# Six weight loads held back in the list that orders a kernel, with new ranks for loads, conversion and masks

## The chip, the cores and the metric

The kernel runs on one core of one Trainium2 chip. The metric is the device time of one execution in microseconds (us). Lines of the kernel (L320) are counted in each kernel's own text, so the same line has a slightly other number in each.

## The reference

```python
# q, k, v: (batch 8, heads 8, seq 576, head_dim 64); tau = 0.02
scores = scale * np.matmul(q, k.transpose(0, 1, 3, 2))
thresh = np.max(scores, axis=-1, keepdims=True) - tau
scores = np.where(scores >= thresh, scores, -1e9)
scores = scores - np.max(scores, axis=-1, keepdims=True)
attn = np.exp(scores); attn = attn / (np.sum(attn, axis=-1, keepdims=True) + 1e-09)
attn_out = np.matmul(attn, v)
# x = attn_out as (8*576, 512); w_in (512, 2048), w_out (2048, 512), given in double precision
h = x @ w_in
out = (h * (1.0 / (1.0 + np.exp(-1.702 * h)))) @ w_out
```

So there are 32 pairs of heads, four to a batch, and 9 blocks of 512 tokens of feed-forward. The first block needs pairs 0 to 3 and the weights. The weights come as 64-bit numbers, and the kernel takes them apart into 32-bit ones on the chip: 32 pieces of 128 x 512, each with two loads of 512 KB, four VectorE operations and one on ScalarE. Pieces 0 to 15 are of w_in, 16 to 31 of w_out.

## The kernel before

The kernel doesn't emit its instructions in the order of the text. It makes a list of tasks with an engine, an assumed cost, a rank, what they come after, and which buffers they take and give. A small loop then plays the list in an assumed time. Whenever an engine is free, it takes the ready task of lowest rank whose buffers are free, and only then is the task's function called, which emits its instructions:

```python
def task(engine, cost, rank, f, *a, after=(), take=(), give=(), lag=0.06):
    ...
    tasks.append((engine, cost, rank, f, a, [x for x in after if x is not None], take, give, lag))
    return len(tasks) - 1
...
            for rank, i in sorted(queue):                 # in run_in_order()
                take = tasks[i][6]
                if all(free[pool] >= take.count(pool) for pool in set(take)):
                    break
            ...
            heapq.heappush(events, (now + tasks[i][1], 0, i))
            tasks[i][3](*tasks[i][4])                      # emits the instructions
```

What comes out is the order of the instructions on each engine. The waits on the chip are put in afterwards, from which instruction writes and reads which buffer.

A piece is converted in one of six places: four quarters of w_out that are not filled yet, and two separate buffers.

```python
def stage(i):                       # STAGES = 4
    if i < n_in:
        return i % (STAGES + 2) if i % (STAGES + 2) < STAGES else None
    ...
for i in range(len(pieces)):
    rank = 3.61 + 0.42 * i / n_in if i < n_in else 4.11 + 0.57 * (i / n_in - 1)
    x = stage(i)
    place = ("w64",) if x is None else (f"stage{x}",)
    a = task("POOL", 2.4, rank, load_w, i, take=place, lag=5.0)
    e = task("DVE", 0.43, rank, cv_ex, i, after=[a])
    m = task("ACT", 0.79, rank, cv_power, i, after=[e])
    a = task("DVE", 1.14, rank, cv_frac, i, after=[e])
    ...
    ready_w.append(task("DVE", 0.7, rank - 1.01, cv_end, i, after=[a, m] + over, give=place))
```

For each pair n, q and k are loaded by SyncE, transposed on VectorE (`prep`), multiplied into scores on TensorE, copied out by ScalarE, and their maxima are taken on VectorE. For the first eight pairs the threshold then goes through DRAM to reach all partitions: `row_out` writes 4.5 KB, `row_in` reads it back spread out to 576 KB and twice 144 KB, and VectorE subtracts it. Masks and exponentials follow on ScalarE.

```python
lq = task("SP", 2.0, r - 2.0, load_qk, n, 0, q0, take=own(n, "raw0"), lag=2.0)
...
pk = task("DVE", 0.77, r, prep, n, 1, after=[lk], take=own(n, "qkT1"), give=own(n, "raw1"))
...
a = task("SP", 0.35, r, row_out, n, after=[a], lag=2.3)
m = task("SP", 1.5, r, row_in, n, after=[a], take=own(n, "mb") + ("mbt",), give=("row",), lag=4.0)
```

Of the kernel before, what the change touches and what calls it, by code (L numbers as in the profile page):

```python
# [30 lines left out]
def kernel(  # L31
# [33 lines left out]
    NKT = 4  # L65
# [18 lines left out]
    psA = ctx.enter_context(tc.tile_pool(name="psA", bufs=3, space=bass.MemoryType.PSUM))  # L84
# [6 lines left out]
    kd = const.tile([P, P], FP32, name="kd")  # L91
    v_t = [const.tile([P, 2, D], FP32, name=f"v_t{i}") for i in range(2)]
# [13 lines left out]

    tasks = []
    limits = {"psA": 3, "psM": 2, "s_m": 8, "s_t": 2, "io": 2, "xT": 3, "mb": 1,
              "raw0": 1, "raw1": 1, "qkT0": 1, "qkT1": 1, "v_m": 2, "w64": 2, "mbt": 1, "row": 1, "kd": 1}
    for x in ("raw0", "raw1", "qkT0", "qkT1", "mb"):  # L110
        limits[x + "_apart"] = 1
    limits["s_m_apart"] = NKT
# [6 lines left out]
        "exps": 0.63,  # L119
        "load_qk": -0.91,  # L120
        "prep": -1.45,
        "load_v": 0.65,
        "over_groups": -1.04,
        "sub": -0.29,
    }
# [2 lines left out]
    def task(engine, cost, rank, f, *a, after=(), take=(), give=(), lag=0.06):  # L128
        if 0 <= rank < LAST:
            rank += (EARLY if a[0] < 2 * NPAIR else LATER).get(f.__name__, 0.0)  # L130
        tasks.append((engine, cost, rank, f, a, [x for x in after if x is not None],
                      take, give, lag))
        return len(tasks) - 1
# [67 lines left out]
    def own(n, *pools):  # L201
        return tuple(x + "_apart" for x in pools) if n in APART else pools
# [33 lines left out]
    n_in = len(pieces)  # L236
# [7 lines left out]
    def stage(i):  # L244

        if i < n_in:
            return i % (STAGES + 2) if i % (STAGES + 2) < STAGES else None
        i -= n_in
        return STAGES - 1 if i % 3 == 0 and i < NFC - PER_STAGE else None
# [281 lines left out]
    def cuts(b):  # L531

        return sorted({0, SH, S} | {x for x in range(-b * S % BLK, S, BLK)})
# [89 lines left out]
    BY_DMA = 8  # L623
    LEAD = 6

    ready_w = []
    for i in range(len(pieces)):
        rank = 3.61 + 0.42 * i / n_in if i < n_in else 4.11 + 0.57 * (i / n_in - 1)
        if not wide:
            ready_w.append(task("POOL", 1.2, rank, load_w, i, lag=2.5))  # L630
            continue
        x = stage(i)
        place = ("w64",) if x is None else (f"stage{x}",)
        a = task("POOL", 2.4, rank, load_w, i, take=place, lag=5.0)
        e = task("DVE", 0.43, rank, cv_ex, i, after=[a])
        m = task("ACT", 0.79, rank, cv_power, i, after=[e])
        a = task("DVE", 1.14, rank, cv_frac, i, after=[e])

        over = [ready_w[y] for y in range(i) if i >= n_in and stage(y) == (i - n_in) // PER_STAGE]
        ready_w.append(task("DVE", 0.7, rank - 1.01, cv_end, i, after=[a, m] + over, give=place))  # L640

    warm = task("ACT", 1.5, -2.0, first_act)
    tau_done = task("DVE", 1.0, -2.0, tau_terms, after=[warm])
# [41 lines left out]
    for n in range(NP):  # L685
        gate = per_pair * (n - LEAD)
        after = ffn[gate : gate + 1] if gate >= 0 else []
        r = float(n)

        slow = 1.2 if n < NPAIR else 1.0  # L690
        q0, q1 = (nc.sync, nc.scalar) if n == 0 else (nc.sync, nc.sync)
        lq = task("SP", 2.0, r - 2.0, load_qk, n, 0, q0, take=own(n, "raw0"), lag=2.0)
        lk = task("SP", 2.0 if n else 0.1, r - 2.0, load_qk, n, 1, q1, take=own(n, "raw1"), lag=2.0)
        lv = task("SP", 2.1, r - 1.2, load_v, n, take=("v_m",), lag=2.0)
        pq = task("DVE", 0.77, r, prep, n, 0, after=[lq], take=own(n, "qkT0"), give=own(n, "raw0"))
        pk = task("DVE", 0.77, r, prep, n, 1, after=[lk], take=own(n, "qkT1"), give=own(n, "raw1"))
        pd = task("ACT", 0.5, r, prep_kd, n, after=[pk], take=("kd",))
        mx = []
        for t in range(NKT + 1):
            tail = t == NKT  # L700
            copies = []
            for c in range(1 if tail else 2):

                a = task(
                    "PE", (0.97 if tail else 0.53) * slow, r, scores, n, t, c,
                    after=[pq, pk] + ([pd] if tail else []) + after,
                    take=("psA", "s_t") if tail else ("psA",) + (own(n, "s_m") if c == 0 else ()),
                    give=own(n, "qkT0", "qkT1") + ("kd",) if tail else (),
                )
                after = [a]  # L710
                copies.append(task("ACT", 0.65, r, keep, n, t, c, after=[a], give=("psA",)))
            mx.append(task("DVE", 0.76 if tail else 1.37, r, in_groups, n, t, ALU.max, after=copies))
        a = task("DVE", 0.78, r, over_tiles, n, ALU.max, after=mx)
        a = task("DVE", 0.78, r, over_groups, n, ALU.max, after=[a])
        if n < BY_DMA:
            a = task("DVE", 0.5, r, lower_rows, n, after=[a, tau_done], take=("row",))
            a = task("SP", 0.35, r, row_out, n, after=[a], lag=2.3)
            m = task(
                "SP", 1.5, r, row_in, n, after=[a], take=own(n, "mb") + ("mbt",), give=("row",),
                lag=4.0,  # L720
            )
        else:
            a = task("DVE", 0.7, r, lower, n, after=[a, tau_done])
            m = task("DVE", 1.38, r, spread_max, n, after=[a], take=own(n, "mb"))
        ws, subs = [], [m]
        for t in range(NKT + 1):
            tail = t == NKT
            a = task(
                "DVE", (0.76 if n < BY_DMA else 1.5) if tail else 1.36, r, sub, n, t, after=subs[-1:],
                give=own(n, "mb") + (("mbt",) if n < BY_DMA else ()) if tail else (),  # L730
            )
            subs.append(a)
            a = task("ACT", 0.68 if tail else 1.16, r, mask, n, t, after=[a])
            ws.append(task("ACT", 0.87 if tail else 1.34, r, exps, n, t, after=[a]))
        back = own(n, "s_m") * NKT + ("s_t",)
        every = range(NKT + 1)
        if n < NPAIR:

            pv = den = None
            for t in every:  # L740
                first = t == 0
                den = task(
                    "PE", 1.1 * slow, r, sums_by_pe, n, [t], True, after=[ws[t], den],
                    take=("psM", "psM") if first else (),
                )
                pv = task(
                    "PE", 1.1 * slow, r, values, n, [t], after=[ws[t], den, pv, lv],
                    take=("psA",) if first else (), give=(back[t],) if t < NKT else ("s_t", "v_m"),
                )
            a = task("DVE", 1.22, r, one_row, n, after=[den], give=("psM", "psM"))  # L750
        else:
            pv = task("PE", 4.85, r, values, n, every, after=ws + [lv], take=("psA",), give=("v_m",))
        if NPAIR <= n < BY_PE:
            a = task("PE", 5.2, r, sums_by_pe, n, every, False, after=ws + [pv], take=("psA",), give=back)
            a = task("DVE", 1.22, r, one_row, n, after=[a], give=("psA",))
        elif n >= BY_PE:
            su = [
                task("DVE", 0.76 if t == NKT else 1.37, r, in_groups, n, t, ALU.add, after=[ws[t]])
                for t in range(NKT + 1)
            ]  # L760
            a = task("DVE", 0.78, r, over_tiles, n, ALU.add, after=su + [pv], give=back)
            a = task("DVE", 0.78, r, over_groups, n, ALU.add, after=[a])
            a = task("DVE", 0.7, r, one_group, n, after=[a])
        a = task("DVE", 1.07, r, spread_sums, n, after=[a])
        b, hp = divmod(n, NPAIR)
        new = {(b * S + x) // BLK for x in cuts(b)[:-1]} if hp == 0 else set()
        if b:
            new -= {(b * S - 1) // BLK}
        placed[n] = task(
            "DVE", 1.1, r, place_x, n, after=[a, pv], take=("xT",) * len(new), give=("psA",)  # L770
        )
        while hp == NPAIR - 1 and (next_blk + 1) * BLK <= (b + 1) * S:
            feed_forward(next_blk)
            next_blk += 1
# [31 lines left out]
```

## Time and profile before

| | before |
|---|---|
| time | 1435.12 us, median of 3 (1434.89 to 1436.98) |
| span of the profiled run | 1431.2 us |
| TensorE busy, idle | 1380.6, 50.6 us |
| of the idle time, in the first 126 us | 41.2 us |
| first feed-forward matmul; pair 3 placed | 117.8; 118.8 us |
| longest wait of VectorE in the front | 11.7 us, for q of pair 1 |

From 240 us to the end TensorE is idle for only 3.9 us. The time is therefore decided in the front, before the first block of feed-forward runs without gaps, and at one later wait for w_out. The lines themselves are in the prediction.

### The profile page before, as it was taken

To read this page: it belongs to the slowest core of one execution; us is meant where nothing else is said; L and a number is where in the kernel's file an instruction comes from. 1 tells how busy PE (TensorE), PEld (TensorE's weight loads), DVE (VectorE), ACT (ScalarE), POOL (GpSimd) and SP (SyncE) were. 2 spreads that over 40 slices of the span, in tenths; PEclk is the share of its full clock that TensorE was granted. 3 is DMA by queue.
4 is the path that set the end of the run, shared out by engine and by line. 5 is a ranking of instruction groups with operands and counts; after the bars stand their busy time and mean duration, and the time that the engine had idled before them with its cause. 6 is when DMAs were issued, how large, how long until landed. Compare 5 with 4: busy or idle time off the path is not lost.

```text
span 1431.2 us, 13710 instructions
## 1 busy us (share of the span) xinstructions
PE 1380.6 (96%) x4936; PEld 650.2 (45%) x4936; DVE 970.2 (68%) x1629; ACT 658.9 (46%) x886; POOL 35.8 (3%) x78
## 2 busy tenths in 40 slices
PE   3779989999999999999999999999999999999998
PEld 2344434444444444444444444444444444444443
DVE  3999999888778888888887887788778710100200
ACT  3786655555455555555555554455445500100100
POOL 2012220000000000000000000000000000000000
PEclk8999999999999999999999999999999999999999
DMA  9468673211111111111111111111110000000000
GB/s 246 99 191 259 204 254 94 67 33 25 33 40 33 26 25 40 33 33 25 33 40 33 25 31 34 40 25 25 33 40 8 1 8 22 0 7 22 0 7 22
DMA packets 205707, 79.31 MB, mean 55 GB/s; under 512 B 192840, under 2 KB 192840, under 8 KB 205640
## 3 DMA queue, kind: packets, MB, share of 16 engines
q1 hardware_dynamic: 196072, 44.60, 14.4%
q0 software_dynamic: 7200, 33.55, 6.6%
q8 instruction: 39, 0.64, 0.2%
q10 hardware_dynamic: 2368, 0.30, 0.1%
q14 instruction: 28, 0.23, 0.1%
HBM read 68.93 MB, written 9.47 MB: 55 GB/s over the span
## 4 chain that ended last, share of the span: by engine, by line
PE 88%; DVE 6%; SPq 2%; DMA 2%; ACT 1%; issue 1%; DVEq 0%; ACTq 0%
PE ops L574 34%; PE hps L555 34%; PE pv L476 9%; PE ps L344 9%; PE ps L337 2%; SPq L214 2%; DVE s_m L447 1%; DVE part L377 1%; DMA mb<-row 1%; ACT gT L462 1%; ACT gT L458 1%; DMA row<-flat 0%; PE den L476 0%; DVE w_in L309 0%; DVE gT L447 0%
## 5 line engine op out<-in xcount | busy, mean ns | idle before, releaser
L574 PE MATMUL ops<-w_out,gT 128*128 128x512 f32 x1152 | 507.8, 596 | 5.0 <-DVE w_out L309 5.0
L555 PE MATMUL hps<-xT,w_in 128*128 128x512 f32 x1152 | 506.4, 595 | 0.3 <-DVE gT L566 0.3
L377 DVE TRANSPOSE_TENSOR_REDUCE part<-s_m 128x36 f32<-128x1152 f32 x228 | 303.5, 1358 | 101.8 <-ACT s_m L363 96.8
L574 PEld LDWEIGHTS ops<-w_out,gT 128*128 128x128 f32 x1152 | 216.2, 190 | 273.8 <-issue 263.5
L555 PEld LDWEIGHTS hps<-xT,w_in 128*128 128x128 f32 x1152 | 216.3, 190 | 267.9 <-issue 256.4
L566 DVE SCALAR_TENSOR_TENSOR gT<-th,hps 128x512 f32<-128x512 f32 x144 | 97.5, 677 | 234.8 <-ACT th L563 234.2
L363 ACT COPY s_m<-ps 128x576 f32<-128x576 f32 x240 | 138.8, 650 | 155.4 <-PE ps L344 153.9
L563 ACT ACTIVATE th<-hps 128x512 f32<-128x512 f32 x144 | 85.2, 592 | 217.4 <-PE hps L555 191.6
L458 ACT ACTIVATE s_m<-s_m 128x1152 f32<-128x1152 f32 x120 | 137.6, 1153 | 62.5 <-DVE s_m L447 62.1
L462 ACT ACTIVATE s_m<-s_m,shift,scl 128x1152 f32<-128x1152 f32 x120 | 160.5, 1343 | 2.4
L447 DVE TENSOR_TENSOR s_m<-s_m,mb 128x1152 f32<-128x1152 f32 x120 | 156.2, 1351 | 5.0 <-DMA mb<-row 4.3
L344 PE MATMUL ps<-qkT 64*128 64x288 f32 x960 | 144.6, 432 | 12.7 <-DVE qkT L320 12.2
L581 ACT ACTIVATE osb<-ops 128x512 f32<-128x512 f32 x36 | 21.4, 594 | 233.5 <-PE ops L574 233.3
L344 PEld LDWEIGHTS ps<-qkT 64*128 64x128 f32 x960 | 83.9, 189 | 91.4 <-issue 52.5
L476 PE MATMUL pv<-s_m,v_m 128*64 128x288 f32 x960 | 124.9, 413 | 0.0
L476 PEld LDWEIGHTS pv<-s_m,v_m 128*64 128x64 f32 x960 | 67.2, 138 | 64.0 <-issue 12.6
L377 DVE TRANSPOSE_TENSOR_REDUCE part_t<-s_t 128x18 f32<-128x576 f32 x59 | 44.2, 749 | 0.7 <-ACT s_t L363 0.2
L543 DVE TENSOR_TENSOR xT<-pv,rc 128x288 f32<-128x288 f32 (+8 forms) x96 | 28.3, 350 | 17.0 <-PE pv L476 15.7
L337 PE MATMUL ps<-qkT,kd 128*128 128x288 f32 x120 | 36.8, 429 | 0.3 <-ACT s_m L363 0.3
L476 PE MATMUL pv<-s_t,v_t 128*64 128x288 f32 x256 | 36.5, 406 | 0.0
L452 DVE TENSOR_TENSOR s_t<-s_t,mb 64x576 f32<-64x576 f32 x48 | 36.0, 749 | 0.3
L325 ACT COPY kd<-qkT 64x64 f32<-64x64 f32 x60 | 14.5, 241 | 45.6 <-DVE qkT L320 45.2
(81 smaller groups left out, 621.4 us busy)
## 6 DMA issues: line engine op xcount, KB each, us to landing
out_dram<-osb SPq DMA_DIRECT2D x36, 256.0 KB, 2.0
q_raw<-in_q_dram SPq DMA_DIRECT2D x120, 72.0 KB, 2.2
k_raw<-in_k_dram SPq DMA_DIRECT2D x116, 72.0 KB, 2.3
v_m<-in_v_dram SPq DMA_DIRECT2D x64, 128.0 KB, 2.4
w_out<-in_moe_w_in_dram POOLq DMA_DIRECT2D x12, 512.0 KB, 9.1
w<-in_moe_w_out_dram POOLq DMA_DIRECT2D x12, 512.0 KB, 4.8
w_out<-in_moe_w_in_dram POOLq DMA_DIRECT2D x12, 511.6 KB, 10.0
w64s<-in_moe_w_out_dram POOLq DMA_DIRECT2D x12, 511.6 KB, 5.8
```

Source lines behind the costliest of these rows:

```text
L337: nc.tensor.matmul(ps[:, i, 0:SH], lhsT=kd, rhs=qT[:, ts(i, SH)], start=True, stop=True,)
L344: nc.tensor.matmul(ps[:, h, 0:SH], lhsT=kT[ts(h, D), ts(t, P)], rhs=qT[ts(h, D), ts(c, SH)], start=True, stop=True,)
L363: nc.scalar.copy(out=o, in_=pss.pop((n, t, c))[:, :, 0:SH])
L377: nc.vector.tensor_reduce(out=o, in_=i, axis=AXL.X, op=op, apply_transpose=True)
L447: nc.vector.tensor_tensor(out=s, in0=s, in1=mb, op=ALU.subtract)
L458: nc.scalar.activation(out=s, in_=s, func=AF.Prelu, alpha=STEEP)
L462: nc.scalar.activation(out=s, in_=s, func=AF.Exp, scale=scl, bias=shift)
L476: nc.tensor.matmul(o[c][ts(h, D), 0:SH], lhsT=lhsT, rhs=rhs, start=(t == 0), stop=(t == NKT),)
L555: nc.tensor.matmul(hidden[j], lhsT=w_in[:, c, ts(j, P)], rhs=xTs[blk][:, c, :], start=(c == 0), stop=(c == NDC - 1),)
L563: nc.scalar.activation(out=ths[j], in_=hidden[j], func=AF.Tanh, scale=GELU_SCALE / 2)
L566: nc.vector.scalar_tensor_tensor(out=gT[j], in0=ths.pop(j), scalar=1.0, in1=hidden.pop(j), op0=ALU.add, op1=ALU.mult)
L574: nc.tensor.matmul(acc[i], lhsT=gT[j][:, ts(i, P)], rhs=w_out[:, j, :], start=(j == 0), stop=(j == NFC - 1),)
```

## The change

Its intent: six weight loads are held back until k of the third and fourth pair (pairs 2 and 3) is transposed, and loads and conversion get other ranks. The mask moves behind the exponentials, and the list learns of three buffers that it did not count.

```diff
-              ... "kd": 1}
+              ... "kd": 1, "rc": 1, "v_t0": 1, "v_t1": 1}
...
-        "load_v": 0.65,
+        "load_v": 1.46,
+        "mask": 1.27,
...
-        rank = 3.61 + 0.42 * i / n_in if i < n_in else 4.11 + 0.57 * (i / n_in - 1)
+        rank = 3.41 + 0.67 * i / n_in if i < n_in else 4.4 + 0.36 * (i / n_in - 1)
...
         a = task("POOL", 2.4, rank, load_w, i, take=place, lag=5.0)
+        w_loads.append(a)
...
-        ready_w.append(task("DVE", 0.7, rank - 1.01, cv_end, i, ...))
+        ready_w.append(task("DVE", 0.7, rank - 2.28, cv_end, i, ...))
...
         pk = task("DVE", 0.77, r, prep, n, 1, after=[lk], ...)
+        if n in (2, 3):
+
+            for a in w_loads[3 * (n - 2) : 3 * (n - 1)]:
+                tasks[a][5].append(pk)
...    (take and give of "rc" and of the tail of v, cut)
```

More of the change, by code (lines that the diff above doesn't have):

```diff
@@ L108 @@
     limits = {"psA": 3, "psM": 2, "s_m": 8, "s_t": 2, "io": 2, "xT": 3, "mb": 1,
-              "raw0": 1, "raw1": 1, "qkT0": 1, "qkT1": 1, "v_m": 2, "w64": 2, "mbt": 1, "row": 1, "kd": 1}
+              "raw0": 1, "raw1": 1, "qkT0": 1, "qkT1": 1, "v_m": 2, "w64": 2, "mbt": 1, "row": 1, "kd": 1, "rc": 1, "v_t0": 1, "v_t1": 1}
     for x in ("raw0", "raw1", "qkT0", "qkT1", "mb"):
@@ L624 @@
     LEAD = 6
-    ready_w = []
+    ready_w, w_loads = [], []
     for i in range(len(pieces)):
-        rank = 3.61 + 0.42 * i / n_in if i < n_in else 4.11 + 0.57 * (i / n_in - 1)
+        rank = 3.41 + 0.67 * i / n_in if i < n_in else 4.4 + 0.36 * (i / n_in - 1)
         if not wide:
@@ L639 @@
         over = [ready_w[y] for y in range(i) if i >= n_in and stage(y) == (i - n_in) // PER_STAGE]
-        ready_w.append(task("DVE", 0.7, rank - 1.01, cv_end, i, after=[a, m] + over, give=place))
+        ready_w.append(task("DVE", 0.7, rank - 2.28, cv_end, i, after=[a, m] + over, give=place))
     warm = task("ACT", 1.5, -2.0, first_act)
@@ L693 @@
         lk = task("SP", 2.0 if n else 0.1, r - 2.0, load_qk, n, 1, q1, take=own(n, "raw1"), lag=2.0)
-        lv = task("SP", 2.1, r - 1.2, load_v, n, take=("v_m",), lag=2.0)
+        v_tail = f"v_t{n % 2}"
+        lv = task("SP", 2.1, r - 1.2, load_v, n, take=("v_m", v_tail), lag=2.0)
         pq = task("DVE", 0.77, r, prep, n, 0, after=[lq], take=own(n, "qkT0"), give=own(n, "raw0"))
         pk = task("DVE", 0.77, r, prep, n, 1, after=[lk], take=own(n, "qkT1"), give=own(n, "raw1"))
+        if n in (2, 3):
+            for a in w_loads[3 * (n - 2) : 3 * (n - 1)]:
+                tasks[a][5].append(pk)
         pd = task("ACT", 0.5, r, prep_kd, n, after=[pk], take=("kd",))
@@ L747 @@
                     "PE", 1.1 * slow, r, values, n, [t], after=[ws[t], den, pv, lv],
-                    take=("psA",) if first else (), give=(back[t],) if t < NKT else ("s_t", "v_m"),
+                    take=("psA",) if first else (), give=(back[t],) if t < NKT else ("s_t", "v_m", v_tail),
                 )
@@ L751 @@
         else:
-            pv = task("PE", 4.85, r, values, n, every, after=ws + [lv], take=("psA",), give=("v_m",))
+            pv = task("PE", 4.85, r, values, n, every, after=ws + [lv], take=("psA",), give=("v_m", v_tail))
         if NPAIR <= n < BY_PE:
@@ L763 @@
             a = task("DVE", 0.7, r, one_group, n, after=[a])
-        a = task("DVE", 1.07, r, spread_sums, n, after=[a])
+        a = task("DVE", 1.07, r, spread_sums, n, after=[a], take=("rc",))
         b, hp = divmod(n, NPAIR)
@@ L769 @@
         placed[n] = task(
-            "DVE", 1.1, r, place_x, n, after=[a, pv], take=("xT",) * len(new), give=("psA",)
+            "DVE", 1.1, r, place_x, n, after=[a, pv], take=("xT",) * len(new), give=("psA", "rc")
         )
```

## The prediction

> **What bounds the kernel now.** I read the page's engine totals and its 40 slices first. One slice is 1431.2 / 40 = 35.8 us.
>
> ```profile
> PE 1380.6 (96%) x4936; PEld 650.2 (45%) x4936; DVE 970.2 (68%) x1629; ACT 658.9 (46%) x886; POOL 35.8 (3%) x78
> ...
> PE   3779989999999999999999999999999999999998
> ...
> DVE  3999999888778888888887887788778710100200
> ```
>
> TensorE is idle for 1431.2 - 1380.6 = 50.6 us in all, and the digits put nearly all of it into the first four slices. Nothing that is done about weights, loads or ranks can shorten the saturated part; it can only shorten the front. So I took the windows of the front (columns: window, its length, then busy us of PE, PEld, DVE, ACT, POOL, then the granted clock, DMA share, GB/s).
>
> ```profile
> 0.00:18.00 18.00, 7.52 (x34) 5.29 (x35) 3.87 (x10) 6.56 (x12) 8.23 (x26) 1.00 0.96 288
> 18.00:36.00 18.00, 6.86 (x36) 4.70 (x35) 8.80 (x17) 6.15 (x13) 0.00 (x0) 0.72 0.85 201
> 36.00:54.00 18.00, 10.69 (x66) 5.76 (x67) 15.46 (x23) 15.28 (x22) 0.00 (x0) 0.91 0.50 109
> 54.00:72.00 18.00, 15.61 (x118) 8.26 (x116) 17.79 (x26) 12.82 (x13) 1.04 (x2) 1.00 0.37 89
> 72.00:90.00 18.00, 12.00 (x82) 6.95 (x80) 16.94 (x29) 14.25 (x23) 1.09 (x3) 0.95 0.68 193
> 90.00:108.00 18.00, 16.62 (x116) 8.37 (x114) 17.37 (x37) 14.62 (x17) 2.12 (x4) 0.86 0.55 183
> 108.00:126.00 18.00, 15.54 (x96) 8.42 (x94) 16.93 (x35) 14.16 (x22) 6.48 (x13) 1.00 0.66 224
> ```
>
> PE is busy for 84.8 of these 126 us, so 41.2 of the 50.6 idle us lie here. There are two regimes. From 36 to 126 us VectorE is the bound: 84.5 of 90 us busy, while it does the maxima and the subtraction for pairs 0 to 3 and the first weight conversions. From 0 to 36 us VectorE itself is starved: 12.7 of 36 us busy, 23.3 us idle, and the DMA engines are at 96% and 85%. The feed-forward matmuls, which then keep TensorE full to the end, need xT of pair 3; VectorE places it at 118.8 us. Time lost by VectorE before 36 us is therefore lost by the whole kernel. The waits of VectorE up to 37 us say for what:
>
> ```profile
> DVE gT L320 <- DMA gT<-in_q_dram: 11.7, 1, 11.7
> DVE neg L607 <- DMA tau_b<-in_tau_dram: 6.0, 1, 6.0
> DVE part L377 <- ACT s_m L363: 2.8, 1, 2.8
> DVE qkT L320 <- DMA q_raw<-in_q_dram: 2.2, 1, 2.2
> DVE gT L320 <- DMA gT<-in_k_dram: 0.3, 1, 0.3
> ```
>
> The big one, 11.7 us, is pair 1's q (pairs 1 and 3 live in the gT space). The chain and the DMA queues in 9 to 27 us show why it is late: SyncE's issue of pair 1's q, normally about 0.5 us for each of four transfers, takes 15.5 us, because the DMA engines are full of weights (queue, packets, MB, share of the 16 engines).
>
> ```profile
> 7.38 7.92 SPq L214
> ...
> 15.34 6.25 SPq L214
> ...
> q0 software_dynamic: 1121, 5.25, 74.3%
> q1 hardware_dynamic: 4662, 0.72, 23.7%
> ```
>
> And these weights are not needed then. Six pieces (two 512 KB transfers each) are fetched by 26 us, one is touched by an 0.39 us operation at 10.35 us, and the rest wait for VectorE: the next weight load waits 56.5 us for a free place, and the first conversion is finished at about 70 us.
>
> ```profile
> 70.96 0.53 POOL L272 DMA_DIRECT2D w_out<-in_moe_w_in_dram  x1 [56.50 <-DVE w_out L283]
> ```
>
> **What the Trainium skill says.** "DMA: Bandwidth & Descriptors", section "Issuing engines are not separate DMA queues": transfers started from SyncE, ScalarE and GpSimd run on the same 16 engines and interleave. The trace agrees: GpSimd's queue took 74.3% of the engines' time, SyncE's 23.7%, and it was SyncE's issue that stretched. The same page, "Queues, rings and completion order", says that an engine takes turns between its queues packet by packet; large weight packets against 128-byte pieces of q and k would then give the weights most of the time, as seen. "TensorE: Matmul & The Clock Gate", Part 1, says that the clock is released after some 3.4 us of sustained work and falls back when idle. The trace agrees: the 32 score matmuls of pair 0 took 7.04 us (220 ns each) and those of pair 1, after an 11.1 us gap, 6.00 us (188 ns), while 12 later ones took 1.73 us (144 ns).
>
> **The change, part by part.**
>
> 1. The hold. The six loads go behind the transpose of k of pair 2 (three) and of pair 3 (three). No instruction is added; bytes and conversions stay. First, pair 0: q and k needed 24.2% + 23.4% of the first 9 us of all engines = 4.3 us of DMA time, and weights took another 40.5%. Without them the pair should land before VectorE's last tau operation ends (6.8 us), so its transposes start at about 6.9 instead of 8.99: 2.1 us. Its scores and copies then take as long as now (from the end of k's transpose at 10.4 to the last copy's end at 19.6: 9.2, less one 0.74 us conversion on ScalarE that no longer lies among them): from 8.3 to about 16.8. Second, pair 1: SyncE reaches its q at 6.6 us as now, issues q and k in 2.06 us each (as for pair 2 now: 26.95 and 29.11) and they land 2.4 us later, at about 13. So its transposes fit into the holes between pair 0's maxima and its scores follow pair 0's on a warm TensorE. Third, VectorE: last maximum 0.73 us, then the reduction to the threshold row, 2.4 us now (32.79 to 34.99) and say 2.9 with waits, then pair 2's transposes 1.4 us: it reaches pair 1's maxima at about 16.8 + 0.7 + 2.9 + 1.4 = 21.9 instead of 36.33. **That is 14.4 us.**
>
> 2. A further 2.06 us idle before the first subtraction now (43.51, waiting for the threshold row from DRAM, 5.5 us of DMA) can go, since VectorE will have pair 1's whole chain to do. But the first three weight loads start at about 22 us and run against just that row: at 147.45, with busy engines, the row took 6.3 us instead of 3.8. I count +1 us of the 2.
>
> 3. Are the weights late now? Pieces 0 to 2 are issued at about 22 us and 3 to 5 at about 30; the landing is 3.6 to 13 us in this trace, so all six are there by about 42. The first conversion moves from 68.5 to about 53. They still wait for VectorE: cost 0.
>
> 4. The new ranks. Finishing a conversion earlier frees its place and so starts the next load earlier; the ranks of w_out, the later v, and the masks behind the exponentials on ScalarE shift order only. They bear on one visible wait:
>
> ```profile
> PE ops L574 <- DVE w_out L309: 5.0, 1, 5.0
> ```
>
> At 208.4 us TensorE outruns the last w_out conversions, whose loads (203.7 to 214.7) wait for conversion places. Earlier finishes argue for less of it; the later rank of w_out (4.4 and on, before 4.11 and on) argues for more. I count +2 us of the 5, and my uncertainty here is 5 us either way.
>
> 5. The extra limits on rc and on the tail of v name buffers that have 1 and 2 copies anyway; they should order nothing differently: 0.
>
> Sum: 14.4 + 1 + 0 + 2 = about 17 us, 1435.1 - 17 = 1418.
>
> **The rivals.** (a) The gain is eaten on the way: the front stays bound by VectorE, but weight loads now start 20 us later and the feed-forward waits for w_in. In favour: 16 pieces, 16.8 MB, before the last first-layer weights; at the 190 to 220 GB/s of the windows that is some 80 us, so from 22 us on they would be all there only at about 102, near the new start of feed-forward (118 - 15). Against: even now only six places are held before 70 us and feed-forward begins with 9 of 16 pieces finished, so the early fetch bought nothing. If true, half the gain: 1427. (b) The conversions come at worse moments after the new ranks: the 5.0 us wait grows to 10 and TensorE gets other holes between 120 and 240 us, where VectorE is still 95% busy. Then 1424 to 1430. (c) The order gets much better than I can see: VectorE's remaining 5.5 us of idle time from 36 to 126 us and the whole 5.0 us stall go too: 1435 - 16.5 - 5 - 4 = 1409. (d) The hold has no effect because pair 1's q was limited by SyncE's own issue of small packets. Against: pair 2's q took 2.06 us when weights had landed. I give it very little; then 1435.
>
> **Range and chances.** The front's 14 us rests on durations in the trace, the rest is order. I take 1418, with 1409 (rival c) to 1428 (rivals a and b). Over 2% faster needs 1406.4, that is 28.7 us, out of 41.2 + 5.6 us of idle TensorE in the first 240 us; VectorE has some 97 us of work to do before feed-forward and cannot begin before 6 us, so feed-forward can hardly begin before 103 instead of 118 unless work is also moved behind it. So 5%. Slower by 2% needs the order to break badly: 1%.
>
> **What would show it.** Right: the 11.7 us wait for pair 1's q is under 1 us; pair 0's first transpose starts at about 7 us and pair 1's maxima at about 22; VectorE is busy for over 22 us in the first 36; feed-forward's first matmul comes at about 102 to 105 us, and TensorE is full from there. Wrong: VectorE's new idle time in 22 to 45 us waiting for the threshold row behind the weights; matmuls of the first layer waiting for w_in conversions; a w_out wait above 5 us; or a feed-forward start that moves by less than 10 us although the front moved by 14.

## More of the kernel before

Every number of a profile comes from one traced execution; every time is a median of several executions.

The weight loads are the only tasks of GpSimd in the list.

## The result, and the profile after

The changed kernel took 1438.2 us (median of 4, 1437.14 to 1439.05), the kernel before 1435.04 us (median of 4). The ratio is 1.0019 with a 95% interval of 1.0001 to 1.0036. A ratio here is the mean time of one kernel's runs over that of the other's of the same rounds, so it is not quite the ratio of the medians. The predicted 17 us did not come; if anything the kernel lost 3. The traced execution of the kernel before took 1433.0 us, 2 us under its median, and that of the changed kernel 1438.75, so differences between these two traces are some 2.5 us larger than those of the medians.

The totals and the slices of the page of the changed kernel:

```profile
PE 1382.0 (96%) x4936; PEld 650.0 (45%) x4936; DVE 970.3 (68%) x1629; ACT 661.3 (46%) x886; POOL 36.1 (3%) x78
...
PE   3779989999999999999999999999999999999998
...
DVE  3888989988888888888887887788777720100100
```

The span is 1436.9 us, so TensorE is idle for 54.9 us: 4.3 more than before, beside 1.4 us more of busy time. The first slice of VectorE is as empty as it was. Its waits up to 37 us (engine, tile and line, what ended the wait, us in total, times, longest) are those of before, within 0.5 us:

```profile
DVE gT L321 <- DMA gT<-in_q_dram: 11.6, 1, 11.6
DVE neg L608 <- DMA tau_b<-in_tau_dram: 6.0, 1, 6.0
DVE part L378 <- ACT s_m L364: 2.8, 1, 2.8
DVE qkT L321 <- DMA q_raw<-in_q_dram: 2.7, 1, 2.7
```

The timeline of GpSimd says why. The first line is its first weight transfer in the kernel before, the next two are the first and the thirteenth of the changed kernel (start, us, engine, line, operation):

```profile
2.46 0.53 POOL L272 DMA_DIRECT2D w_out<-in_moe_w_in_dram  x1
...
2.46 0.53 POOL L273 DMA_DIRECT2D w_out<-in_moe_w_in_dram  x1
...
75.15 0.54 POOL L273 DMA_DIRECT2D w_out<-in_moe_w_in_dram  x1 [60.46 <-DVE w_out L284]
```

The first weight load still starts at 2.46 us, the same hundredth as before. Six pieces are fetched at once, and the seventh waits 60.5 us for a place. No load was held back. Printing the list as it is played for both kernels shows what the new rule did instead. This is the order of the pieces on GpSimd:

```
before: 0 1 2 3 4 5 6 7 8 9 10 11 12 13 14 15 17 18 16 ...
after:  6 7 8 9 10 11 0 1 12 2 13 14 3 4 5 15 17 18 16 ...
```

Only pieces 0 to 5 were told to come later. At time 0 all six places were free and GpSimd was idle, so the list gave the places to pieces 6 to 11, whose place rule (i modulo 6) fits. On the chip nothing makes these loads wait: GpSimd's queue begins with them. The six loads moved from early to early, under other names.

The windows of the front (length, then busy us of PE, PEld, DVE, ACT, POOL, then granted clock, DMA share, GB/s) show the two small losses:

```profile
0.00:18.00 18.00, 6.97 (x36) 4.58 (x36) 3.87 (x10) 6.89 (x13) 8.23 (x26) 1.00 0.94 289
18.00:36.00 18.00, 5.61 (x29) 4.33 (x28) 8.14 (x16) 4.71 (x10) 0.00 (x0) 0.62 0.83 197
...
90.00:108.00 18.00, 11.48 (x80) 6.04 (x76) 14.48 (x34) 12.95 (x21) 4.08 (x8) 0.96 0.79 234
```

In the first 36 us VectorE is busy for 12.0 us (before: 12.7) under a DMA share of 94% and 83%. Between 90 and 108 us it is busy for 14.5 us, where it had 17.4. Over the first 126 us TensorE is idle for 43.3 us (before 41.2). Pair 3 is placed at 123.6 us instead of 118.8, and the first feed-forward matmul comes at 126.7 us instead of 117.8. The wait for the last w_out conversions is still there:

```profile
PE ops L575 <- DVE w_out L310: 5.6, 1, 5.6
```

### The profile page after: what moved, and what is told of

Same layout as the page of the kernel before. It is cut to its first block, busy times and chain, and to the rows that moved or that the text cites. A ratio compares the mean times of both kernels' runs of the same rounds, so it can differ in the third digit from the quotient of the medians.

```text
span 1436.9 us, 13707 instructions
## 1 busy us (share of the span) xinstructions
PE 1382.0 (96%) x4936; PEld 650.0 (45%) x4936; DVE 970.3 (68%) x1629; ACT 661.3 (46%) x886; POOL 36.1 (3%) x78
## 4 chain that ended last, share of the span: by engine, by line
PE 88%; DVE 5%; DMA 3%; SPq 2%; ACT 1%; issue 1%; DVEq 0%; ACTq 0%
PE hps L556 34%; PE ops L575 33%; PE pv L477 10%; PE ps L345 8%; PE ps L338 2%; SPq L215 2%; DVE part L378 1%; DVE s_m L448 1%; DMA w64s<-in_moe_w_in_dram 1%; PE den L477 1%; DMA mb<-row 1%; DMA row<-flat 0%; DMA gT<-row 0%; ACT gT L459 0%; ACT s_m L463 0%
## 5 line engine op out<-in xcount | busy, mean ns | idle before, releaser
L544 DVE TENSOR_TENSOR xT<-pv,rc 128x288 f32<-128x288 f32 (+8 forms) x96 | 28.3, 350 | 17.4 <-PE pv L477 15.9
L422 DVE STREAM_TRANSPOSE mb<-thr 128x1152 f32<-128x1152 f32 x24 | 33.1, 1377 | 0.7
```

## The experiments

Theory 1: the hold is a rule of the list only; it did not hold anything on the chip, and it swapped pieces. The prediction's mechanism (late weights free the DMA engines for q and k) was never tried. Rivals: it is the new ranks that took the gain away; or a real hold would gain nothing, because the weights would then be late or VectorE is stuck for another reason. Printed like those above, the lists of e3, e5 and e6 give every engine the same order of tasks, and so do those of e4, e8, e9, e10 and e11. Within each group only the wait on the chip differs, with GpSimd's short copy that makes it, so e6 and e9 are the controls for all real holds. Twelve kernels were run in three rounds each; all results were correct. Times are medians of 4; before had 1435.07, 1435.08 and 1435.96 us.

| run | edit | us | ratio to before (95%) |
|---|---|---|---|
| e1 | hold in the list alone | 1442.5 | 1.0053 (1.0038 to 1.0068) |
| e2 | new ranks alone | 1437.99 | 1.0019 (1.0002 to 1.0036) |
| e3 | before, hold on the chip | 1428.85 | 0.9957 (0.9942 to 0.9972) |
| e4 | changed, hold on the chip | 1430.83 | 0.9971 (0.9956 to 0.9985) |
| e5 | before, hold behind rows 0 and 1 | 1422.55 | 0.9909 (0.9893 to 0.9926) |
| e6 | e3's order, no wait on the chip | 1433.26 | 0.9987 (0.9972 to 1.0002) |
| e7 | mask rank alone | 1437.81 | 1.0019 (1.0004 to 1.0034) |
| e8 | changed, hold behind rows 0 and 1 | 1420.83 | 0.9904 (0.9889 to 0.9918) |
| e9 | changed, old order of pieces | 1436.11 | 1.0001 (0.9983 to 1.0018) |
| e10 | changed, all six behind row 1 | 1422.57 | 0.9906 (0.9891 to 0.9921) |
| e11 | changed, behind rows 1 and 2 | 1424.41 | 0.9918 (0.9903 to 0.9933) |
| e12 | before, pair 1's transposes later | 1434.82 | 0.9992 (0.9976 to 1.0008) |

**e1_hold_only** adds only the hold to the kernel before:

```diff
+        w_loads.append(a)
...
+        if n in (2, 3):
+            for a in w_loads[3 * (n - 2) : 3 * (n - 1)]:
+                tasks[a][5].append(pk)
```

> The kernel before with the hold of the change alone, no other rank. Theory 1 (the hold is only a rule of the list that sets the order; pieces 6 to 11 take the six free places at time 0 and pieces 0 to 5, which the first feed-forward matmuls need, come last): no weight load starts later on the chip, VectorE still waits about 11.6 us for q of pair 1, the first loads are of pieces 6 to 11, and the kernel is slower than before by some 3 to 6 us (1438 to 1441). Theory 2 (the ranks are what costs): as before, 1435 within 1 us.

It took 1442.5 us, 7.4 us more. Its first weight load starts at 2.46 us and VectorE waits 11.8 us for q of pair 1. The list's order is 6 7 8 9 10 11 0 1 12 13 2 3 4 5. Theory 1 holds, and the loss is larger than expected. The largest part of it is a wait of TensorE, which was one of 5.0 us before:

```profile
PE ops L574 <- DVE w_out L309: 10.3, 2, 7.4
```

**e2_ranks_only** is the changed kernel without its hold (the four added lines at `if n in (2, 3)` taken out).

> The changed kernel without its hold: all new ranks and limits, weight pieces in their old order 0 to 31. Theory 1 (order of the pieces costs): at or below the kernel before, 1431 to 1436. Theory 2 (the ranks cost): like the changed kernel, about 1438. Both: the 11.6 us wait for q of pair 1 stays.

It took 1437.99 us, like the changed kernel. Here theory 1's number was a miss, since it expected at most 1436: the ranks cost about 3 us by themselves (0.3 to 5 us by the interval).

**e6_ordered_before** is e1 with the pieces kept in order, still without a wait on the chip:

```diff
+        w_loads.append(a)
+        if i >= 6:
+            tasks[a][5].append(w_loads[5])
```

> Control for e3: the same order of all instructions by the list (pieces 0 to 31 in order, six loads held in the list alone), no wait on the chip. Weight loads start at 2.5 us as in the kernel before and the 11.6 us wait for q of pair 1 stays. If the wait on the chip is the whole of e3's gain, this is 1435 within 3 us; if the order of the conversions gave it, about 1429.

It took 1433.26 us, the same as before within the interval, and 9.2 us less than e1. The two differ in the order of the pieces and in what the list makes of it elsewhere, so the swap cost e1 its time. The w_out wait is 4.7 us here and 10.3 in e1, which is 5.6 of the 8.0 us between the two profiled spans. How the swapped pieces lead to the longer wait I did not follow further.

**e9_ordered_after** makes the same two-line addition to the changed kernel.

> The changed kernel with loads from 6 on kept behind load 5 in the list, so that pieces come in the order 0 to 31 again; still no wait on the chip. It closes the square of e1, e6, e7 and the changed kernel. If the swapped order of the pieces costs 9 us (e1 against e6) also beside the new ranks, this is below 1431; if the new ranks have taken that cost up (the changed kernel is only as slow as e2 and e7), it is 1435 to 1438.

It took 1436.11 us against 1438.2 of the changed kernel; the two intervals overlap. Beside the new ranks the swap costs 2 us or nothing, not 9. The two parts of the change do not add up: 7.4 for the hold and 3 for the ranks give 3 together.

**e7_mask_only** gives the kernel before one new line, `"mask": 1.27,`.

> The kernel before with the mask's rank alone (masks behind exponentials, so mask and exponential alternate by tile). If this rank makes the 3 us of e2, about 1438, with pair 3's place at about 123 us and more TensorE idle at the w_out wait; if the ranks of loads, conversion and v make it, 1435 within 1 us.

It took 1437.81 us, so this rank alone costs as much as all new ranks together, within the noise (0.6 to 5 us). In the list, masks and exponentials of a pair now alternate tile by tile. On the chip pair 3 is placed at 121.7 us instead of 118.8, and the w_out wait grows:

```profile
PE ops L575 <- DVE w_out L310: 7.6, 2, 7.3
```

**e3_real_before** makes the hold real. GpSimd copies one column of the transposed k in its own queue ahead of the loads. The copy reads a buffer that VectorE writes, so it waits on the chip, and the loads stand behind it in order. The two lines of e6 keep the other pieces behind.

```diff
         mats[n, which] = dst
+        if which == 1 and n in (2, 3):
+            nc.gpsimd.tensor_copy(out=held[:, n - 2 : n - 1], in_=dst[:, 0:1])
```

> The kernel before with a hold that is real on the chip: GpSimd copies one column of the transposed k of pair 2 and of pair 3, in its own queue ahead of weight loads 0 to 2 and 3 to 5, and loads from 6 on stay behind them. The prediction's mechanism: the wait for q of pair 1 falls under 1 us, pair 1's maxima start at about 22 us, feed-forward starts 10 to 15 us earlier, 1420 to 1425. Rival (weights become late, or conversions wait for them): feed-forward waits for w_in conversions and the kernel is at 1428 or above.

It took 1428.85 us: 6 us gained, where the prediction's first part counted 14.4. That is the rival's number, but not its reason: TensorE shows no wait for a w_in conversion. The weights come late, as asked, and pair 1's q is issued quickly. First the kernel before, SyncE's issue of that q, then e3, the same issue and GpSimd's first weight transfer:

```profile
6.62 15.51 SPq L214 DMA_DIRECT2D gT<-in_q_dram  x4
...
5.87 2.07 SPq L215 DMA_DIRECT2D gT<-in_q_dram  x4
...
22.86 0.53 POOL L273 DMA_DIRECT2D w_out<-in_moe_w_in_dram  x1 [0.29 <-issue]
```

Up to 22 us the prediction's own numbers come out. The timeline of VectorE for pair 0's first transpose and pair 1's maxima, in the kernel before (L320, L377) and in e3, and e3's next long wait:

```profile
8.99 0.78 DVE L320 STREAM_TRANSPOSE qkT<-q_raw 128x576 f32<-128x576 f32 x1 [2.16 <-DMA q_raw<-in_q_dram]
...
36.33 5.11 DVE L377 TRANSPOSE_TENSOR_REDUCE part<-gT 128x36 f32<-128x1152 f32 x4
...
7.04 0.78 DVE L321 STREAM_TRANSPOSE qkT<-q_raw 128x576 f32<-128x576 f32 x1
...
22.15 5.11 DVE L380 TRANSPOSE_TENSOR_REDUCE part<-gT 128x36 f32<-128x1152 f32 x4
...
56.40 1.36 DVE L450 TENSOR_TENSOR gT<-gT 128x1152 f32<-128x1152 f32 x1 [11.96 <-DMA gT<-row]
```

I had worked out 6.9 and 21.9 us; measured are 7.04 and 22.15 (before: 8.99 and 36.33). VectorE is busy for 24.3 of the first 36 us. Then the wait comes back in another place. Of the 14.2 us gained, 12.0 are lost waiting for pair 1's threshold row. Feed-forward was expected to start 10 to 15 us earlier and does not: pair 3 is placed at 117.4 us (before 118.8, e6 122.0), and the first matmul comes at 120.1 us. The timeline of SyncE's queue shows the same jam as before, one stage later:

```profile
25.19 10.11 SPq L215 DMA_DIRECT2D q_raw<-in_q_dram  x4
35.34 5.64 SPq L215 DMA_DIRECT2D k_raw<-in_k_dram  x4
41.08 0.36 SPq L432 DMA_DIRECT2D row<-flat  x1
52.26 0.36 SPq L441 DMA_DIRECT2D gT<-row  x1
```

Loads 0 to 2 start at 22.9 us. SyncE, which is just issuing pair 4's q and k (not needed before 65 us), needs 15.8 us for what takes 4.1 us when no weights are in flight. So the row, ready at 37.9 us, is issued only at 41.1. By then loads 3 to 5 run (from 39.6 us), and the 4.5 KB take 11.2 us to pass. Since e6 has the same order of tasks and its gain of some 2 us is not clear of zero, the wait on the chip made most of e3's gain: 4.4 us between these two medians, 4.6 between their spans.

**e4_real_after** is the same in the changed kernel: the prediction as it was meant.

> The changed kernel with the same real hold and the pieces in their old order. The prediction as it was meant: 1418, that is 14 to 20 us below before. Rival: the new ranks cost a few us against e3 (then e3 is faster by over 2 us), or late weights take half the gain (1427).

It took 1430.83 us: 1418 is missed by 13 us. It is 2 us above e3, but the two intervals overlap. Its long wait is 10.8 us for the same row. The rival "late weights take half the gain" (1427) has neither the number nor the mechanism: it is the row that comes late, not w_in.

**e5_rows_before** puts the loads between the rows. GpSimd's copy reads the row that has landed, for pair 0 (loads 0 to 2) and pair 1 (loads 3 to 5):

```diff
         nc.sync.dma_start(out=mb, in_=row.to_broadcast([P, 2 * S]))
+        if n in (0, 1):
+            nc.gpsimd.tensor_copy(out=held[:, n : n + 1], in_=mb[:, 0:1])
...
+            if n in (0, 1):
+                for x in w_loads[3 * (n - 0) : 3 * (n - 0 + 1)]:
+                    tasks[x][5].append(m)
```

> As e3, but weight loads 0 to 2 wait for the threshold row of pair 0 and loads 3 to 5 for that of pair 1 (GpSimd copies one column of the row that has landed), so they fall between the rows and not on them. If the 12.0 us wait of VectorE for pair 1's row, with SyncE's issue of pair 4's q and k stretched to 10.1 and 5.6 us, is what ate the gain of e3, this wait falls under 3 us and the kernel comes 7 to 11 us below e3: 1418 to 1422. Rival (VectorE's or the weights' work bounds the front anyway): within 3 us of e3, 1426 to 1429.

It took 1422.55 us, 0.6 us above the expected range and 6.3 below e3 instead of 7 to 11. The wait only fell from 12.0 to 5.1 us and not under 3, and a new one of 6.6 us for the row of pair 2 stands beside it. (The four executions spread from 1420.45 to 1426.05 us, and the traced one is the slowest.) Against e6, its control, e5 gains 10.7 us. It differs from e3 only in where the weights wait, so their place had cost e3 6.3 us.

**e8_rows_after** is the same hold in the changed kernel.

> The hold of e5 in the changed kernel. If the new ranks cost 2 to 3 us wherever they stand (e2 against before, e4 against e3), this is 2 to 3 us above e5: 1420 to 1425. If they were tuned for loads that come late, at or below e5.

It took 1420.83 us, 14.3 us below before and 17.4 us below the changed kernel. It is the fastest version tried, though its interval overlaps those of e5, e10 and e11. The ranks that cost 3 us with early loads show no cost here. In the profiled runs (span 1420.4 against 1431.2) the idle time of TensorE up to 126 us falls from 41.2 to 28.4 us, and the first feed-forward matmul comes at 111.25 us. Between 126 and 240 us it rises from 5.6 to 8.3 us, mostly at one place. First the wait as the profile names it, then the matmul behind it, then VectorE's timeline at that moment:

```profile
PE ops L578 <- DMA q_raw<-in_q_dram: 7.3, 1, 7.3
```

```profile
200.96 2.08 PE L578 MATMUL ops<-w_out,gT 128*128 128x512 f32 x2 [7.31 <-DMA q_raw<-in_q_dram]
```

```profile
200.22 0.68 DVE L311 SCALAR_TENSOR_TENSOR w_out<-w64s,w 128x512 f32<-128x512 int32 x1
```

These matmuls read w_out, not q. The conversion that writes a piece of w_out ends at 200.90 us and the matmul starts at 200.96. It is the old w_out wait, put down to a transfer that came late in the same moment. The hold did not make it longer. e9, which has the same order of tasks and no hold on the chip, has it as well:

```profile
PE ops L575 <- DVE w_out L310: 8.3, 2, 7.3
```

The wait follows the order of the list: 4.6 to 5.1 us in before, e3, e5 and e6, 7.6 to 8.4 in the seven runs that have the mask's new rank and the pieces in their old order (e2, e4 and e7 to e11). Orders that differ more give 9.0 (e12) and 10.3 us (e1). With the hold everything up to it only moves: the second layer starts at 182.3 us in e8 and at 195.9 in e9, 13.6 us earlier, and the span of the profiled run is 13.5 us shorter. So the wait on the chip alone makes e8's gain.

**e10_row1_after** lets all six loads wait for pair 1's row (`if n == 1`, `w_loads[:6]`); **e11_row12_after** uses rows 1 and 2 (`if n in (1, 2)`).

> As e8, but all six loads wait for pair 1's row. In e8 VectorE still waited 4.5 us for that row, which shared the DMA engines with loads 0 to 2. If this wait is on the path, it goes and the kernel is 3 to 5 us below e8: 1416 to 1418. If the weights become late instead, or the wait for w_out conversions (8.3 us in e8) grows by as much, it is at e8 or above: 1420 to 1424.

> Loads 0 to 2 behind pair 1's row, loads 3 to 5 behind pair 2's. Rival of e10: weights can be held too long. If so, feed-forward waits for w_in conversions and this is slower than e10 by 3 us or more; if the front is bound by VectorE alone, equal to e10 within 2 us.

They took 1422.57 and 1424.41 us. In e10 the wait for pair 1's row is gone, as intended, and a like one has appeared at pair 2's:

```profile
DVE s_m L451 <- DMA mb<-row: 4.7, 1, 4.7
```

So e10's expected 3 to 5 us did not come. Its number lies in the second range, but for neither reason named there: the w_out wait is 7.8 us (8.3 in e8), and no w_in conversion shows a wait of over 1.0 us in either run. e11 is 1.8 us above e10, within the 2 us of "equal"; its wait stands before pair 3's row, with 6.6 us. In e5, e8, e10 and e11 alike, one or two waits of 4.5 to 6.6 us for some row remain. The rows of e8 and e10 run beside the six held pieces; the two waits of 6.6 us, in e5 and e11, stand beside loads of the pieces after them, which start at 68.5 and 79.9 us.

**e12_prep_late** leaves the weights alone and takes pair 1's transposes out of the way of pair 0's maxima:

```diff
-        pq = task("DVE", 0.77, r, prep, n, 0, ...)
+        rp = 2.0 if n == 1 else r
+        pq = task("DVE", 0.77, rp, prep, n, 0, ...)     # pk likewise
```

> The kernel before, weights not held, with pair 1's transposes ranked behind pair 0's maxima, so that VectorE's program order no longer puts the q that is late ahead of work that is ready. If the 11.7 us wait costs so much because VectorE takes its work in a fixed order, about half of it comes back: 1428 to 1431. If pair 1's late data alone sets the front, as before: 1434 to 1436.

It took 1434.82 us, as before. The 11.7 us wait fell to 4.3, but other waits for q and k of pairs 0 to 2 came up (4.4, 1.7 and 1.3 us), the w_out wait is 9.0 us instead of 5.0, and pair 3 is placed at 119.2 us instead of 118.8. Undoing VectorE's fixed order at this one place gained nothing, and the waits that remain are for the data of the next pairs. The edit also moves other tasks of the list, so this argues for late data as what sets the front; e3 against e6 shows it.

## Why the prediction was wrong

1. **The step that failed is "1. The hold": "The six loads go behind the transpose of k of pair 2 (three) and of pair 3 (three)."** I read a line that adds an entry to a task's list of predecessors as a wait on the chip. It is none. It only changes the order in which the list is played, and GpSimd, which has nothing but weight loads to order, starts its first six from 2.46 us on, as before. It did not even move loads in the order of the list to a later place, because it held pieces 0 to 5 and not the places, and pieces 6 to 11 took them. Both could be read from `run_in_order` and from `stage` before the run. All of the 14.4 us hung on it. Rival (d), "The hold has no effect" (1435), comes near the number, but its reason is wrong: in e3 SyncE issues pair 1's q in 2.07 us.

2. **The mechanism behind it was right up to 22 us**, as e3 shows: 22.15 us against 21.9 worked out. GpSimd's weights and SyncE's q and k run on the same DMA engines (the Trainium skill, "DMA: Bandwidth & Descriptors", "Issuing engines are not separate DMA queues"), and the runs agree: without weights, pair 1's q and k were issued in 2.07 and 2.12 us instead of 15.5 and 4.7. Slips in the working change little: 16.8 + 0.7 + 2.9 + 1.4 is 21.8, from 32.79 to 34.99 is 2.2 us and not 2.4, and VectorE is 92% busy from 120 to 240 us, not 95%. For the clock only pair 1 agrees as said: its matmuls ran at a granted 0.50 from 29.8 to 33.4 us and at 1.00 after that. For pair 0 the record shows 1.00 throughout, so what made its matmuls slow (220 ns each) is open.

3. **Step 2 was mis-sized.** I saw that the loads would run against a threshold row and counted 1 us of loss. In e3 the wait for pair 0's row is 2.0 us, as before, so the 1 us of gain did not come, and the loss is 12.0 us, at pair 1's row. I had left out that SyncE's own issue stalls, so the row waits in its queue behind q and k of pair 4. I had named a wait for the threshold row behind the weights among the things that would prove me wrong, for 22 to 45 us; it stood at 44 to 56 us.

4. **Step 3 held**: with a real hold of up to 51 us (e8) no w_in conversion waited for more than 1.0 us. Rival (a), late w_in, falls. Only its time was off: VectorE's first conversion starts at 66.6 us in e3 and at 59.2 in e8, not at 53.

5. **Step 4 was wrong in sign.** I counted 2 us of gain at the w_out wait. It went from 5.0 to 5.6 us in the changed kernel, to 7.6 with the mask's rank alone (e7), and to 8.3 in e8 and e9. The new ranks cost about 3 us as they stand (e2), the mask's alone as much (e7); that is the direction of rival (b). In step 5 the extra limits were never run by themselves, so their cost is open.

6. **The sum of 17 us** is not far from what the hold can give when it is real and stands in the right place: e8 gained 14.3 us. That is partly luck: e8 holds the loads behind other events, and its gain is what is left beside a row wait of 4.5 us and a w_out wait of 8.3 that the sum did not have.

## What to carry to other kernels

A rule in a program that orders instructions is not a wait on the chip. Before counting on it, ask which instruction would wait for which buffer, and look whether the queue concerned has anything else to do first. When something is held back from a shared resource, hold all that can take its place, and check what it will run against when it is let go: here (e3) 3 MB of weights that nobody waited for ran beside a 4.5 KB row that VectorE waited for. A gain measured at one point of the front is only kept if the next hand-over isn't in the way of the moved work.

## What the Trainium skill lacked or had wrong

- "DMA: Bandwidth & Descriptors", "Issuing engines are not separate DMA queues", says that issuing from several engines saves only the sequencer's time for the issue, "which is usually small relative to the DMA itself". Here the issue itself was the loss: one 72 KB transfer of q that is issued in 0.5 us took 7.92 us to issue while weights filled the engines, and in e3 eight such issues took 15.8 instead of 4.1 us. Everything behind them in SyncE's queue waited too. The page does not say that an issuing engine can be stalled by another engine's transfers.
- The same page, "Anatomy of one DMA", gives some 2 us of fixed cost for a small transfer on GpSimd's path. No page says how long a small one takes behind large ones: the 4.5 KB row from SyncE took 1.7 us in the kernel before and 11.2 us in e3, beside 3 MB of weights.
- "Perfetto Trace Analysis", "Optimization Strategy", advises to find the gaps and what they wait for, so as to make those dependencies start sooner. It lacks the case in which the cure moves the same wait: 11.7 us for q of pair 1 became 12.0 us for the row of pair 1 (e3), then 4.5 us for the same row (e8) and 4.7 us for the row of pair 2 (e10).
